# Single-bank PSUM tiles after the attention, and attention inputs in 128 partitions, in a linear-attention kernel with two MLPs

## The chip, the cores and the metric

The kernel runs on one core of a Trainium2 chip. The metric is the device time of one execution in microseconds (us). Three executions of the kernel before were timed; the profile comes from one more.

## The reference

Inputs: q, k, v of shape (4, 8, 576, 64), a scale g_norm of 64, and four weight matrices; all float32. Cut to what is computed:

```
kv  = einsum('bhsd,bhse->bhde', k, v)
o   = einsum('bhsd,bhde->bhse', q, kv)
x   = o / sqrt(mean(o*o, -1) + 1e-6) * g_norm      # as (2304 tokens, 512)
h   = x @ w_in;   h = softplus(h);        x = h @ w_out     # 512 -> 2048 -> 512
h   = x @ w_in2;  h = max(0.01*h, h);     out = h @ w_out2  # 512 -> 2048 -> 512
```

## The kernel before

**Attention.** There are four batches of 576 positions and four head pairs each, so 16 units. For a unit u, `load(u)` issues three DMAs from SP that bring q, k and v of two heads into `lda`, six neighbouring positions a partition in 96 partitions (`PQ = 96`, `R6 = 6`), in a ring of four buffers (`NLD = 4`). `T(u)` copies q into another order (`qp`, L372 to L376), transposes it in six pieces on TensorE (L419), forms k^T v of both heads in twelve small matmuls (L426), and evacuates both (`kvm` L436, `qt` L451 to L453). `O(u)` multiplies `qt` by `kvm` (L467) and copies the result into `xy` (L475, L477). `norm(b)` and `X(u)` scale a batch once its four pairs are there (L495 to L552).

**The MLPs.** Each of the two matrix products of each MLP is done as seven block products on sums of blocks (a Strassen-like scheme), with every operand split into a high and a low part, so that a block product is six matmuls. `product` (L820) does the first product of an MLP in pieces of six 384-column matmuls, `piece` (L1077, 256 columns; L1082, 384 columns) the second. `plain` (L910) does the first few blocks without the scheme, while the attention still runs. ScalarE and VectorE evacuate each piece: L1127, L1134, L1139, L841 and L835 after `product`, L699, L694 and L1093 after `piece`; L849 and L854 split the results for the next product.

**PSUM.** The eight banks of 512 float32 are allocated as four tiles `pw0` to `pw3` of 1024 columns, two banks each, for the whole kernel. `ps[0]` to `ps[7]` are the halves of these. `product` writes U into bank 0 or 1, V into bank 2 and W into bank 3 (`u_bank`); in `after`, L1139 copies U into W. `piece` writes banks 4 and 5, or 6 and 7. So two banks of one tile are in use for different pieces at the same time.

**What sets the order.** A planner (`Plan`) gets every operation with its cost by engine, the bank or the part of a buffer that it reads and writes (banks as keys `("ps", 0)` to `("ps", 7)`), and a due time; it makes a list schedule, and the code is emitted in that order, engine by engine. The waits between engines are added afterwards by the tile framework from what each instruction reads and writes in its tiles; they don't come from the planner's keys.

Of the kernel before, what the change touches and what calls it, by code (L numbers as in the profile page):

```python
# [133 lines left out]
def linear_attention_two_mlps(  # L134
# [32 lines left out]
    nc = tc.nc  # L167
# [6 lines left out]
    R6 = 6  # L174
    PQ = S // R6
# [168 lines left out]
    both = mstp.tile([P, 4, 8], F32, name="both")  # L344
    nc.gpsimd.memset(ones, 0.0)
# [47 lines left out]
    def load(u):
        b, hp = u // NPAIR, u % NPAIR
        hs = slice(2 * hp, 2 * hp + 2)
        for nm, src in (("q", q), ("k", k), ("v", v)):
            def fn(e, nm=nm, src=src):
                nc.sync.dma_start(
                    out=lda[nm][u % NLD],
                    in_=src[b, hs].rearrange("h (p r) d -> p h r d", r=R6),  # L400
                )

            op({"S": 0.93}, fn, (), [(nm, u % NLD)])

# [52 lines left out]
    o_, s_of = pw[2][:, 0:S], pw[2][:, S:S + HS]  # L457
# [33 lines left out]
    def norm(b):  # L491
        def f_s(e):
            for w in range(NB):
                for c in range(4):
                    nc.tensor.matmul(  # L495
                        s_of[32 * c:32 * (c + 1), :], ones[:, 6 - 2 * w:38 - 2 * w],
# [4 lines left out]
        sk, rk = [("ps", 5)], [("rs", b % 2)]  # L501
# [3 lines left out]
            lambda e: nc.scalar.activation(fa, s_of, AF.Ln, bias=eps_b, scale=2.0 ** -SHIFT / D),  # L505
# [7 lines left out]
        for w, (x, s0, o0) in enumerate(  # L513
            ((s_of, D * EPS, ALU.add), (fm, 1.0 / D, ALU.mult), (fm, -3.0, ALU.add))
# [23 lines left out]
    def X(u):  # L538
# [10 lines left out]
        op({"PE": 0.28}, f_b, [("rs", b % 2), ("pick",)], RK)  # L549
# [10 lines left out]
    def decode_w(F, which, a_reg):  # L560
# [22 lines left out]
        op({"S": (1.65, 1.4)[which]}, f_l, after_loads if (which, f) < (1, GF) and which else (), rk)  # L583
# [754 lines left out]
```

## Time and profile before

| | before |
|---|---|
| timed, median of 3 (us) | 847.48 (846.77 to 848.55) |
| the profiled execution's own time (us) | 847.53 |
| its span, first to last instruction (us) | 845.7 |
| TensorE matmul busy (us) | 802.2 |
| TensorE weight load busy (us) | 757.1 |
| VectorE / ScalarE busy (us) | 679.0 / 538.2 |
| mean granted TensorE clock | 0.988 |

A matmul's end is modelled in this profile, so the matmul row can look busy across part of a wait; the weight loads of the same engine have a row of their own (PEld). An idle time is given in brackets before the group that it precedes, with what ended it.

### The profile page before, as it was taken

The numbers are of one execution on the slowest core, as the hardware profiler recorded it, in microseconds if no ns is written. First come the engines' busy times: TensorE is split into PE (matmuls) and PEld (weight loads), VectorE is DVE, ScalarE is ACT, GpSimd is POOL, SyncE is SP. The second block draws the span as 40 slices with busy tenths as digits, with TensorE's granted clock in tenths as the row PEclk, the third lists the DMA queues.
The fourth block names the chain that finished last, engine by engine and source line by source line (L and its number), as shares of the span: only waits on it lengthen the run. The fifth ranks groups of instructions, "written<-read, shape, count | busy, mean of one in ns | idle before, by whom it ended". The sixth has DMA issues, their size and how long they took to land. (4 is left out here: it accounts for less than half of the span.)

```text
span 845.7 us, 13740 instructions
## 1 busy us (share of the span) xinstructions
PE 802.2 (95%) x5309; PEld 757.1 (90%) x5309; DVE 679.0 (80%) x1036; ACT 538.2 (64%) x883; POOL 41.0 (5%) x38
## 2 busy tenths in 40 slices
PE   7899799899999999999999999999999999999996
PEld 6677799898999999999998988998999999999996
DVE  3785899898888987886798998898889876876565
ACT  2587679778667675764467787686577554454441
POOL 2340620000000000000000000000000000000000
PEclk9999799999999999999999999999999999999999
DMA  9995448476854874754676959774865752563814
GB/s 250 269 260 193 193 180 321 177 247 251 327 209 186 311 254 164 289 198 155 247 269 223 349 187 404 273 266 151 331 216 187 295 206 104 213 211 107 280 39 112
DMA packets 71250, 192.53 MB, mean 228 GB/s; under 512 B 5520, under 2 KB 45456, under 8 KB 71184
## 3 DMA queue, kind: packets, MB, share of 16 engines
q1 hardware_dynamic: 69504, 190.86, 64.8%
q8 instruction: 41, 0.67, 0.3%
q10 hardware_dynamic: 1680, 0.79, 0.3%
q14 instruction: 25, 0.20, 0.1%
HBM read 152.31 MB, written 39.32 MB: 227 GB/s over the span
## 5 line engine op out<-in xcount | busy, mean ns | idle before, releaser
L820 PE MATMUL pw<-ra 128*128 128x384 f32 x1932 | 391.2, 337 | 9.7 <-ACT pw L1139 6.9
L820 PEld LDWEIGHTS pw<-ra 128*128 128x128 f32 x1932 | 332.5, 189 | 16.3 <-ACT pw L1139 10.5
L1077 PE MATMUL pw<-rb 128*128 128x256 f32 x1512 | 209.5, 284 | 9.5 <-DVE xy L699 6.9
L1082 PE MATMUL pw<-rb 128*128 128x384 f32 x1008 | 208.0, 341 | 9.0 <-DVE xy L699 3.8
L1077 PEld LDWEIGHTS pw<-rb 128*128 128x128 f32 x1512 | 195.2, 189 | 22.3 <-DVE xy L699 17.2
L1082 PEld LDWEIGHTS pw<-rb 128*128 128x128 f32 x1008 | 176.3, 189 | 19.4 <-DVE xy L699 11.0
L699 DVE TENSOR_TENSOR xy<-pw,xy 128x384 f32<-128x384 f32 (+2 forms) x247 | 134.1, 549 | 73.6 <-PE pw L1077 50.2
L849 ACT ACTIVATE rb<-mf 128x768 fp32r<-128x768 f32 x154 | 129.5, 845 | 78.5 <-PE pw L1077 41.0
L854 DVE TENSOR_TENSOR rb<-mf,rb 128x768 fp32r<-128x768 f32 x154 | 148.0, 962 | 21.6 <-ACT rb L849 21.1
L934 DVE TENSOR_TENSOR mf<-mf 128x768 f32<-128x768 f32 x68 | 65.7, 975 | 2.8 <-ACT mf L835 2.2
L1127 ACT ACTIVATE mf<-pw 128x384 f32<-128x384 f32 x92 | 44.8, 489 | 35.3 <-PE pw L820 34.3
L1134 DVE TENSOR_TENSOR mf<-pw,mf 128x384 f32<-128x384 f32 x92 | 50.7, 553 | 11.5 <-PE pw L820 10.0
L1139 ACT ACTIVATE pw<-pw 128x384 f32<-128x384 f32 x46 | 22.0, 479 | 25.6 <-PE pw L820 25.1
L835 ACT ACTIVATE mf<-mf 128x768 f32<-128x768 f32 x26 | 21.9, 843 | 18.7 <-DVE mf L1134 18.6
L1093 ACT ACTIVATE pw<-pw 128x384 f32<-128x384 f32 (+2 forms) x44 | 21.0, 478 | 16.1 <-PE pw L1077 9.0
L996 ACT ACTIVATE rb<-rc 128x512 fp32r<-128x512 f32 x44 | 27.3, 626 | 2.0 <-PE pw L1077 0.8
L999 DVE TENSOR_TENSOR rb<-rc,rb 128x512 fp32r<-128x512 f32 x42 | 28.4, 683 | 0.3 <-ACT rb L996 0.3
L841 ACT ACTIVATE mf<-mf 128x768 f32<-128x768 f32 x24 | 20.2, 841 | 8.6 <-DVE mf L1134 8.5
L694 ACT ACTIVATE xy<-pw 128x384 f32<-128x384 f32 (+2 forms) x40 | 18.8, 480 | 10.1 <-PE pw L1077 4.5
L841 ACT ACTIVATE mf<-pw 128x384 f32<-128x384 f32 x32 | 15.7, 491 | 11.5 <-PE pw L820 11.1
L612 ACT ACTIVATE sqr<-mf 128x512 uint16<-128x512 uint16 x29 | 22.6, 780 | 0.0
L475 ACT ACTIVATE xy<-pw 128x576 f32<-128x576 f32 x14 | 9.0, 646 | 21.3 <-PE pw L467 21.2
(120 smaller groups left out, 740.0 us busy)
## 6 DMA issues: line engine op xcount, KB each, us to landing
ra<-xscr SPq DMA_DIRECT2D x131, 768.0 KB, 6.3
xscr<-ra SPq DMA_DIRECT2D x30, 768.0 KB, 4.5
mf<-in_moe_w_in_dram SPq DMA_DIRECT2D x18, 512.0 KB, 5.9
mf<-in_moe_w_out_dram SPq DMA_DIRECT2D x18, 512.0 KB, 4.9
lf<-in_moe_w_in_dram SPq DMA_DIRECT2D x14, 512.0 KB, 6.2
lf<-in_moe_w_out_dram SPq DMA_DIRECT2D x14, 512.0 KB, 5.4
xscr<-xy SPq DMA_DIRECT2D x8, 768.0 KB, 6.3
qa<-in_q_dram SPq DMA_DIRECT2D x16, 288.0 KB, 8.7
```

Source lines behind the costliest of these rows:

```text
L699: {"D": t_d(n)}, lambda e: nc.vector.tensor_tensor(dst, src, dst, ALU.add),
L820: nc.tensor.matmul(o, w_[:, a, c:c + P], e_[:, b, kk, :], start=(not on and which < 2 and kk == 0 and n == 0), stop=(kk == 1 and n == 2), ...
L841: lambda e: nc.scalar.activation(dst(), src(), AF.Prelu, alpha=0.01),
L849: {"A": t_a(n)}, lambda e: nc.scalar.activation(g[:, 0, :, :], c.ap, AF.Copy),
L854: lambda e: nc.vector.tensor_tensor(g[:, 1, :, :], c.ap, g[:, 0, :, :].bitcast(F32), ALU.subtract),
L934: lambda e: nc.vector.tensor_tensor(to.ap, x.ap, y.ap, ALU.subtract),
L996: op({"A": t_a(512)}, lambda e: nc.scalar.activation(w_[:, 0], src(), AF.Copy), sk, hk)
L999: lambda e: ENG[e].tensor_tensor(w_[:, 1], src(), w_[:, 0].bitcast(F32), ALU.subtract), sk + hk, lk,
L1077: nc.tensor.matmul(y[:, 256 * (j % 2):256 * (j % 2 + 1)], G_[:, a, m, js], w_[:, b, m, :], **flags)
L1082: nc.tensor.matmul(y[:, :BN], w_[:, a, m, js], G_[:, b, m, :], **flags)
L1127: {"A": t_a(BN)}, lambda e: nc.scalar.activation(c[:, m, :], src, AF.Copy),
L1134: lambda e: nc.vector.tensor_tensor(c[:, m, :], src, c[:, m, :], ALU.add),
```

## The change

1. **PSUM.** `pw0` to `pw3` stay for the attention alone. They are allocated in two pools, `psb` with `pw1` and `psa` with the other three. When the last unit that uses `pw1` is done (`U_H = 10`), `psb` is closed and banks 2 and 3 become tiles `ps2` and `ps3` of one bank each; when the attention's last norm is done, `psa` is closed and the other six banks become `ps0`, `ps1` and `ps4` to `ps7`. A new tile waits for the users of the old tile that it lies on. What reads a bank in the MLPs looks the tile up when it is emitted (`lambda` and `src()` in place of slices made at the start).
2. **q, k and v.** 512 of the 576 positions of a batch lie in 128 partitions, four to a partition; the 64 that are left come for all eight heads of a batch in one DMA for each of q, k and v (`ldr`, 64 partitions, 256 bytes a row; the other 64 partitions are set to zero once). A unit has four transposes and one for the left rows (`f_tl`), and ten small matmuls in place of twelve. The ring has five buffers.
3. **O and the stores.** In odd batches the 64 left positions stand first in `o_`, so that a matmul's output stays within a bank; the rows of the result are stored in runs of 128 and 64 in place of 96.
4. **The planner's costs** of the loads follow the new sizes, and those of the weights' loads go from 1.65 and 1.4 to 1.47 and 1.3. The block products' costs are as before.

The diff, cut to its core (`psum` slices that became lookups are shown once):

```
-    R6 = 6
-    PQ = S // R6
+    RL = S - 4 * P
...
-        rows = out[b * S:(b + 1) * S, :].rearrange("(p r) d -> r p d", r=R6)
-        runs += [(PQ, rows[r]) for r in range(R6)]
+        rows = out[b * S:b * S + 4 * P, :].rearrange("(p r) d -> r p d", r=4)
+        left = (RL, out[b * S + 4 * P:(b + 1) * S, :])
+        runs += [left] * (b % 2) + [(P, rows[r]) for r in range(4)] + [left] * (1 - b % 2)
...
-    psum = ctx.enter_context(tc.tile_pool(name="psum", bufs=1, space=PSUM))
-    pw = ring(psum, "pw", 4, [P, 1024])
-    ps = [t[:, c:c + 512] for t in pw for c in (0, 512)]
+    psa = tc.tile_pool(name="psa", bufs=1, space=PSUM, side="right")
+    psb = tc.tile_pool(name="psb", bufs=1, space=PSUM)
+    psap, psbp = psa.__enter__(), psb.__enter__()
+    pw = [(psbp if i == 1 else psap).tile([P, 1024], F32, name=f"pw{i}") for i in range(4)]
+    ps = [None] * 8
+
+    def banks(old, name, which, **kw):
+        old.__exit__(None, None, None)
+        p = ctx.enter_context(
+            tc.tile_pool(name=name, bufs=1, space=PSUM, reuse_waits="tile", **kw)
+        )
+        for i in which:
+            ps[i] = p.tile([P, 512], F32, name=f"ps{i}")
...
-    NLD = 4
+    NLD = 5
     NB = 4
     HS = S // 4
-    lda = {nm: ring(attp, nm + "a", NLD, [PQ, 2, R6, D]) for nm in "qkv"}
-    qp = ring(attp, "qp", 2, [PQ, R6, 2, D])
+    lda = {nm: ring(attp, nm + "a", NLD, [P, 2, 4, D]) for nm in "qkv"}
+    ldr = {nm: ring(attp, nm + "r", 2, [P, H, D]) for nm in "qkv"}
+    qp = ring(attp, "qp", 2, [P, 4, 2, D])
...
+    for t, e_ in enumerate((nc.vector, nc.gpsimd)):
+        for n in "qkv":
+            e_.memset(ldr[n][t][RL:], 0.0)
...
-                    in_=src[b, hs].rearrange("h (p r) d -> p h r d", r=R6),
-                )
-
-            op({"S": 0.93}, fn, (), [(nm, u % NLD)])
+                    in_=src[b, hs, 0:4 * P, :].rearrange("h (p r) d -> p h r d", r=4),
+                )
+
+            first = "qkv".index(nm) - 60.0 if u == 0 else None
+            op({"S": 0.74}, fn, (), [(nm, u % NLD)], due=first)
+        if hp == 0:
+            for nm, src in (("q", q), ("k", k), ("v", v)):
+                def fn(e, nm=nm, src=src):
+                    nc.sync.dma_start(
+                        out=ldr[nm][b % 2][:RL], in_=src[b, :, 4 * P:S, :].rearrange("h p d -> p h d")
+                    )
+
+                op({"S": 0.6}, fn, (), [(nm + "r", b % 2)])
...
         t = i if u < U_H else 0
         k0, k1 = ("ps", 2 * t), ("ps", 2 * t + 1)
-        qc = pw[t][:, 32:32 + S]
-        kv = pw[t][:, 32 + S:32 + S + D]
+        qc, kv = pw[t][:, 0:S], pw[t][:, 5 * P:5 * P + D]
         ka, va = lda["k"][u % NLD], lda["v"][u % NLD]
+        ql, kl, vl = (ldr[nm][b % 2] for nm in "qkv")
 
         def f_t(e):
-            for r in range(R6):
-                nc.tensor.transpose(
-                    qc[:, r * PQ:(r + 1) * PQ], qp[i][:, r, :, :], ident[0:PQ, 0:PQ]
-                )
+            for r in range(4):
+                nc.tensor.transpose(qc[:, r * P:(r + 1) * P], qp[i][:, r, :, :], ident)
+
+        def f_tl(e):
+            nc.tensor.transpose(pw[t][:, 4 * P:5 * P], ql[:, h2, :], ident)
 
         def f_kv(e):
-            for r in range(R6):
+            for r in range(5):
                 for h in range(2):
+                    k_, v_ = (x[:, 2 * hp + h, :] for x in (kl, vl)) if r == 4 else (
+                        x[:, h, r, :] for x in (ka, va)
+                    )
                     nc.tensor.matmul(
-                        kv[h * D:(h + 1) * D, :], ka[:, h, r, :], va[:, h, r, :],
-                        start=(r == 0), stop=(r == R6 - 1), tile_position=(0, h * D),
+                        kv[h * D:(h + 1) * D, :], k_, v_, start=(r == 0), stop=(r == 4),
+                        tile_position=(0, h * D),
                     )
 
-        op({"PE": 0.5}, f_t, [("qp", i)], [k0, k1])
-        op({"PE": 0.75}, f_kv, [("k", u % NLD), ("v", u % NLD)], [k1])
+        op({"PE": 0.44}, f_t, [("qp", i)], [k0])
+        op({"PE": 0.11}, f_tl, [("qr", b % 2)], [k1])
+        op(
+            {"PE": 0.7}, f_kv,
+            [("k", u % NLD), ("v", u % NLD), ("kr", b % 2), ("vr", b % 2)], [k1],
+        )
...
+    def o_of(b):
+        return pw[2][:, 4 * P - RL:] if b % 2 else pw[2][:, 0:S]
+
+    def s_of(b):
+        return pw[2][:, 0:HS] if b % 2 else pw[2][:, S:S + HS]
...
-            for c0, c1 in ((0, 512), (512, S)):
-                nc.tensor.matmul(
-                    o_[:, c0:c1], kvm[i], qt[i][:, c0:c1], start=True, stop=True
-                )
+            at = b % 2 * RL
...
-        sk, rk = [("ps", 5)], [("rs", b % 2)]
+        sk, rk = [("ps", 5 - b % 2)], [("rs", b % 2)]
...
-        op({"S": (1.65, 1.4)[which]}, f_l, after_loads if (which, f) < (1, GF) and which else (), rk)
+        op({"S": (1.47, 1.3)[which]}, f_l, after_loads if (which, f) < (1, GF) and which else (), rk)
...
-        U, V, W = (ps[u_bank(s, x_)][:, :BN] for x_ in range(3))
+        U, V, W = (lambda x_=x_: ps[u_bank(s, x_)][:, :BN] for x_ in range(3))
...
+        banks(psa, "psc", (0, 1, 4, 5, 6, 7), side="right")
...
+        if i == U_H:
+            op({"N": 0.0}, lambda e: banks(psb, "psd", (2, 3)), (), [("ps", 2), ("ps", 3)])
...
+       + [("ps", i) for i in (0, 1, 4, 5, 6, 7)]
```

TensorE where the second MLP's second product begins (`pw2` and `pw3` hold banks 4 to 7, `pw0` and `pw1` banks 0 to 3). Before:

```order
L1065 MATMUL pw3_86<-rb_911 128x128 [waits DVE_49]
L1077 MATMUL pw2_85<-rb_911 128x256 [waits DVE_49]
L1077 MATMUL pw2_85<-rb_911 128x256 x11
L820 MATMUL pw1_84<-ra_74 128x384 [waits DMAHW4_49,DVE_49]
L820 MATMUL pw1_84<-ra_74 128x384 x5
L1077 MATMUL pw2_85<-rb_911 128x256 [waits Activation_49]
L1077 MATMUL pw2_85<-rb_911 128x256 x5
L820 MATMUL pw0_83<-ra_74 128x384 [waits DMAHW0_49]
```

Now, with the lines of the changed kernel (L864 is `product`, L1126 is `piece`):

```order
L1114 MATMUL ps6_978<-rb_879 128x128 [waits DVE_49]
L1126 MATMUL ps4_976<-rb_879 128x256 [waits DVE_49]
L1126 MATMUL ps4_976<-rb_879 128x256 x11
L864 MATMUL ps2_561<-ra_74 128x384 [waits DMAHW0_49,DVE_49]
L864 MATMUL ps2_561<-ra_74 128x384 x5
L864 MATMUL ps0_974<-ra_74 128x384 [waits DMAHW4_49,Activation_49]
L864 MATMUL ps0_974<-ra_74 128x384 x5
L1126 MATMUL ps5_977<-rb_879 128x256 [waits DVE_49]
```

The third piece of L1077 writes bank 5; before it waits for ScalarE (for L1093, which reads bank 4 of the same tile), now for VectorE, and a piece of the first product stands ahead of it.

SP's queue from the start, before (`qa`, `ka`, `va` are the ring of `load`):

```order
L398 DMA qa0_93<-in_q_dram 96x2x384
L398 DMA ka0_97<-in_k_dram 96x2x384
L398 DMA va0_101<-in_v_dram 96x2x384
L398 DMA qa1_94<-in_q_dram 96x2x384
L398 DMA ka1_98<-in_k_dram 96x2x384
L398 DMA va1_102<-in_v_dram 96x2x384
L398 DMA qa2_95<-in_q_dram 96x2x384
```

Now (`qr`, `kr`, `vr` hold the left rows):

```order
L412 DMA qa_96<-in_q_dram 128x2x256
L412 DMA ka_101<-in_k_dram 128x2x256
L412 DMA va_106<-in_v_dram 128x2x256
L422 DMA qr_111<-in_q_dram 64x8x64
L422 DMA kr_113<-in_k_dram 64x8x64
L422 DMA vr_115<-in_v_dram 64x8x64
L412 DMA ka_102<-in_k_dram 128x2x256
L412 DMA va_107<-in_v_dram 128x2x256
```

The three loads of left rows stand ahead of the second unit's, and the first unit needs all six.

## Rows read from the trace of the kernel before

**Rows 1.** Busy time of each engine: us (share of the span) xinstructions

```profile
PE 802.2 (95%) x5309; PEld 757.1 (90%) x5309; DVE 679.0 (80%) x1036; ACT 538.2 (64%) x883; POOL 41.0 (5%) x38
```

**Rows 2.** Timeline at the end: start us, us, engine, line, operation [idle before]

```profile
840.37 0.98 PE L1077 MATMUL pw<-rb 128*128 128x256 f32 x6 [0.52 <-DVE xy L699]
```

**Rows 3.** Waits of TensorE's matmuls: engine line <- releaser: us, times, longest us

```profile
PE pw L820 <- ACT pw L1139: 6.9, 10, 2.4
PE pw L1077 <- DVE xy L699: 6.9, 13, 0.8
PE pw L426 <- DMA va<-in_v_dram: 4.6, 5, 1.2
PE pw L1082 <- DVE xy L699: 3.8, 5, 1.4
PE pw L1082 <- DVE rb L854: 2.4, 2, 1.9
...
PE pw L1082 <- ACT xy L694: 1.3, 2, 1.0
```

**Rows 4.** Waits of the weight loads, same columns

```profile
PEld pw L1077 <- DVE xy L699: 17.2, 31, 1.1
...
PEld pw L820 <- DVE mf L1134: 2.3, 2, 1.8
```

**Rows 5.** Timeline near 610 us, columns as in the second group

```profile
607.46 1.59 PE L1077 MATMUL pw<-rb 128*128 128x256 f32 x12
...
608.89 1.21 PE L820 MATMUL pw<-ra 128*128 128x384 f32 x6
...
609.93 0.87 PE L1077 MATMUL pw<-rb 128*128 128x256 f32 x6
...
610.64 1.21 PE L820 MATMUL pw<-ra 128*128 128x384 f32 x6
...
611.65 0.68 DVE L699 TENSOR_TENSOR xy<-pw,xy 128x512 f32<-128x512 f32 x1
...
612.38 1.69 PE L1077 MATMUL pw<-rb 128*128 128x256 f32 x12 [0.53 <-DVE xy L699]
...
613.91 1.21 PE L820 MATMUL pw<-ra 128*128 128x384 f32 x6
```

**Rows 6.** Timeline near 100 us, same columns

```profile
100.35 1.34 PE L820 MATMUL pw<-ra 128*128 128x384 f32 x6 [2.36 <-ACT pw L1139]
```

**Rows 7.** Stretches: busy of PE, PEld, DVE, ACT, POOL; PEclk, DMA, GB/s

```profile
5.50:42.00 36.50, 29.74 (x362) 22.45 (x361) 20.15 (x37) 15.88 (x30) 8.95 (x8) 0.95 1.08 272
42.00:91.20 49.20, 46.44 (x467) 38.70 (x465) 33.99 (x58) 38.54 (x70) 14.88 (x11) 0.94 0.75 212
91.20:480.00 388.80, 372.99 (x2068) 358.16 (x2069) 339.92 (x496) 270.00 (x439) 14.24 (x7) 0.99 0.66 240
480.00:820.00 340.00, 329.83 (x2252) 315.43 (x2251) 267.53 (x411) 207.74 (x340) 0.00 (x0) 1.00 0.61 220
820.00:845.70 25.70, 19.14 (x150) 18.25 (x148) 15.78 (x28) 4.72 (x6) 0.00 (x0) 0.94 0.45 122
```

**Rows 8.** Wait of VectorE for TensorE, columns as in the third group

```profile
DVE xy L699 <- PE pw L1077: 50.2, 64, 1.8
```

**Rows 9.** Groups, first 92 us: operation xcount | busy us, mean ns | idle

```profile
L426 PE MATMUL pw<-va,ka 96*64 96x64 f32 x384 | 14.7, 226 | 4.6 <-DMA va<-in_v_dram 4.6
...
L419 PE MATMUL pw<-ident,qp 96*128 96x96 f32 x96 | 11.3, 255 | 2.5 <-ACT qt L451 0.9 <-POOL qp L376 0.8 <-ACT qp L372 0.4
...
L376 POOL TENSOR_SCALAR qp<-qa 96x768 f32<-96x768 f32 x7 | 5.8, 831 | 27.6 <-DMA qa<-in_q_dram 23.0 <-DVE kvm L436 2.8 <-DVE ra L677 1.8
```

**Rows 10.** Three more stretches, columns as in the seventh group

```profile
5.50:37.00 31.50, 24.74 (x320) 18.70 (x320) 15.18 (x31) 13.60 (x25) 6.46 (x7) 1.00 1.08 272
...
98.00:105.00 7.00, 2.71 (x10) 2.29 (x11) 7.00 (x7) 4.12 (x8) 4.44 (x2) 0.79 0.80 334
832.00:845.70 13.70, 7.99 (x63) 7.37 (x61) 5.61 (x13) 0.00 (x0) 0.00 (x0) 0.89 0.42 115
```

More of the change, by code (lines that the diff above doesn't have):

```diff
@@ L385, in fn @@
             if e == "A":
-                nc.scalar.activation(out, in_, AF.Copy)
+                nc.scalar.activation(out, in_(), AF.Copy)
             else:
-                nc.vector.tensor_copy(out, in_)
+                nc.vector.tensor_copy(out, in_())
         return op({"A": t_a(n), "D": t_d(n)}, fn, [], [("ps", bank), *writes])
@@ L463, in O @@
         cols = slice(b * S, (b + 1) * S)
+        o_ = o_of(b)
         def f_o(e):
-            for c0, c1 in ((0, 512), (512, S)):
-                nc.tensor.matmul(
-                    o_[:, c0:c1], kvm[i], qt[i][:, c0:c1], start=True, stop=True
-                )
+            at = b % 2 * RL
+            nc.tensor.matmul(
+                o_[:, at:at + 4 * P], kvm[i], qt[i][:, 0:4 * P], start=True, stop=True
+            )
+            at = (1 - b % 2) * 4 * P
+            nc.tensor.matmul(
+                o_[:, at:at + RL], kvm[i], qt[i][:, 4 * P:S], start=True, stop=True
+            )
         op({"PE": 0.98}, f_o, [("kvm", i), ("qt", i)], OK)
@@ L491, in norm @@
     def norm(b):
+        s_ = s_of(b)
         def f_s(e):
@@ L513, in norm @@
         for w, (x, s0, o0) in enumerate(
-            ((s_of, D * EPS, ALU.add), (fm, 1.0 / D, ALU.mult), (fm, -3.0, ALU.add))
+            ((s_, D * EPS, ALU.add), (fm, 1.0 / D, ALU.mult), (fm, -3.0, ALU.add))
         ):
@@ L547, in f_b @@
                 )
-        op({"PE": 0.28}, f_b, [("rs", b % 2), ("pick",)], RK)
+        op({"PE": 0.47}, f_b, [("rs", b % 2), ("pick",)], RK)
         op(
@@ L692, in to_xy @@
                 {"D": t_d(n), "A": t_a(n)},
-                lambda e: nc.vector.tensor_copy(dst, src) if e == "D"
-                else nc.scalar.activation(dst, src, AF.Copy),
+                lambda e: nc.vector.tensor_copy(dst, src()) if e == "D"
+                else nc.scalar.activation(dst, src(), AF.Copy),
                 [("ps", bank)], xk,
@@ L698, in to_xy @@
             op(
-                {"D": t_d(n)}, lambda e: nc.vector.tensor_tensor(dst, src, dst, ALU.add),
+                {"D": t_d(n)}, lambda e: nc.vector.tensor_tensor(dst, src(), dst, ALU.add),
                 [("ps", bank)] + xk, xk,
@@ L900, in plain, with o @@
         for m in range(2):
-            o = ps[2 + m][:, :BN]
+            def o(m=m):
+                return ps[2 + m][:, :BN]
             for j in range(2):
@@ L1044, in to_y, with src @@
                 dst = xy[:, 2 * a:2 * a + 2, c0:c0 + n].rearrange("p a (j n) -> p j a n", n=P)
-                src = ps[bank][:, (j0 % 2) * 256:(j0 % 2) * 256 + 2 * n]
-                src = src.rearrange("p (j a n) -> p j a n", a=2, n=P)
+                def src():
+                    y = ps[bank][:, (j0 % 2) * 256:(j0 % 2) * 256 + (j1 - j0) * 256]
+                    return y.rearrange("p (j a n) -> p j a n", a=2, n=P)
                 kcs, n = [2 * a, 2 * a + 1], 2 * n
@@ L1049, in to_y @@
                 kcs, n = [2 * a + j0], BN
-                dst, src = xy[:, kcs[0], c0:c0 + BN], ps[bank][:, :BN]
+                dst, src = xy[:, kcs[0], c0:c0 + BN], lambda: ps[bank][:, :BN]
             to_xy(dst, src, n, g % NG == 0 and i in ((5, 1, 2, 6) if pre else (0, 1, 2, 6)), bank, xyk(kcs, c0, n // len(kcs)))
@@ L1057, in piece @@
             bank = (6 if i in (1, 3, 5) else 4) + (j // 2 if tokens else j)
-            y = ps[bank]
             new = i < 2 or not pre and i == 5
@@ L1063, in fn @@
             def fn(e):
+                y = ps[bank]
                 if widens:
@@ L1092, in piece @@
                         {"A": t_a(n)},
-                        lambda e: nc.scalar.activation(ps[bank + 2][:, :n], y[:, :n], AF.Copy),
+                        lambda e: nc.scalar.activation(
+                            ps[bank + 2][:, :n], ps[bank][:, :n], AF.Copy
+                        ),
                         [("ps", bank)], [("ps", bank + 2)],
@@ L1126, in copy @@
             op(
-                {"A": t_a(BN)}, lambda e: nc.scalar.activation(c[:, m, :], src, AF.Copy),
+                {"A": t_a(BN)}, lambda e: nc.scalar.activation(c[:, m, :], src(), AF.Copy),
                 bank, ck(c, m),
@@ L1133, in plus @@
                 {"D": t_d(BN)},
-                lambda e: nc.vector.tensor_tensor(c[:, m, :], src, c[:, m, :], ALU.add),
+                lambda e: nc.vector.tensor_tensor(c[:, m, :], src(), c[:, m, :], ALU.add),
                 bank + ck(c, m), ck(c, m),
@@ L1138, in after @@
         if i == 0:
-            op({"A": t_a(BN)}, lambda e: nc.scalar.activation(W, U, AF.Copy), bu, bw)
+            op({"A": t_a(BN)}, lambda e: nc.scalar.activation(W(), U(), AF.Copy), bu, bw)
         elif i == 1:
@@ L1149, in after @@
         elif i == 5:
-            act(s, lambda: cA[:, 1, :], lambda: W, BN, bw, ck(cA, 1))
+            act(s, lambda: cA[:, 1, :], W, BN, bw, ck(cA, 1))
         else:
-            act(s, lambda: cA[:, 0, :], lambda: U, BN, bu, ck(cA, 0))
+            act(s, lambda: cA[:, 0, :], U, BN, bu, ck(cA, 0))
     def attention_done(e):
@@ L1182, in warm @@
         for _ in range(N_WARM):
-            nc.tensor.transpose(ps[7][:, 0:P], ident, ident)
+            nc.tensor.transpose(pw[3][:, 512:512 + P], ident, ident)
     op({"PE": 0.0}, warm, (), [("ps", 7)], due=-100.0)
@@ L1229, in linear_attention_two_mlps @@
        + [(t, i) for t in ("qp", "qt", "kvm") for i in range(2)]
-       + [(t, i) for t in "qkv" for i in range(NLD)])
+       + [(t, i) for t in "qkv" for i in range(NLD)]
+       + [(t + "r", i) for t in "qkv" for i in range(2)])
     op({"N": 0.0}, norm_done, (), granules("rc", "lf")
+       + [("ps", i) for i in (0, 1, 4, 5, 6, 7)]
        + [("sq", i) for i in range(NB)] + [("rs", i) for i in range(2)]
```

12 lines of the change are left out of this document (6 added, 6 removed).

## The prediction, made before the changed kernel ran

> **What bounds the kernel now.** I read the busy times first, then the waits of the busiest engine, then one stall closely, then the stretches. TensorE's matmuls are busy 802.2 of 845.7 us, VectorE 679.0 [rows 1]: the kernel is bound by TensorE, and only what lets TensorE lose less, or work less, can move its time. From 91.2 us to the last matmul (the last group starts at 840.37 and takes 0.98, so to 841.35 [rows 2]) it works at the MLPs; before that lies the attention.
>
> What TensorE waits for in the MLPs is nearly all PSUM. Seven rows of its waits name a reader of PSUM, from L820 behind L1139 (6.9 us) to L1082 behind L694 (1.3 us); they add up to 23.5 us [rows 3]. The two waits for an operand, L1082 behind L854, are 2.4 us, and the loads of v cost 4.6 us in the attention. The weight loads show the same stalls larger: six rows, from 17.2 to 2.3 us, 83 waits, 46.7 us in all [rows 4].
>
> The timeline shows which is right. Undisturbed, six matmuls of L820 take from 608.89 to 609.93, 1.04 us, and twelve of L1077 from 607.46 to 608.89, 1.43 us. At the stall six of L820 start at 610.64 and the next group only at 612.38, 1.74 us later, and its twelve take 1.53 us [rows 5]. So the stall costs 0.70 + 0.10 = 0.80 us, where the matmul row shows 0.53 idle: 0.27 us more than is shown, since the modelled end covers a part and the second matmul after a stall is late too. The Trainium skill, Perfetto Trace Analysis, Identifying the Most-Contended Engine, says that matmul busy time is no good measure of the room that is left, and to take the weight loads' busy share; this stall agrees. By the matmul row the room in PSUM waits would be 23.5 us, by the weight loads 46.7.
>
> **Whose bank is it?** In this stall TensorE writes bank 7 (the last third of a `piece`), and what it waits for is L699, which reads bank 6 from 611.65 to 612.33 [rows 5]: the other half of `pw3`. The long one at 100.35 is V, bank 2, behind L1139, which writes W, bank 3; 2.36 us [rows 6]. The planner keeps banks apart, but the waits are made per tile, and a tile has two banks. In the built program, 327 of TensorE's waits in the two products name a user of the other bank of the pair, 74 one of its own bank; in the changed program none and 441. Going through the idle times, 22.5 of the 23.5 us lie behind the other bank; the rest is behind the bank's own reader and stays.
>
> **Part 1, single-bank tiles: what goes.** 22.5 us of shown idle, and 0.27 us for each of 83 waits, 22.4 us: 45 us (46.7 by the weight loads alone). I share it out by the weight loads' idle: 388.8 - 358.2 = 30.6 us from 91.2 to 480, 340 - 315.4 = 24.6 from 480 to 820, 21.35 - 18.25 = 3.1 from there to the last matmul [rows 7]. That makes 23.6, 19.0 and 2.4 us.
>
> **What is late next.** A stall that goes brings TensorE to its next need sooner. VectorE is the engine that could then be late: it is busy 339.9 of 388.8 us in the first stretch and 267.5 of 340 in the second [rows 7]. With the stalls gone these shares would be 339.9/365.2 = 93% and 267.5/321 = 83%. That is near the limit in the first. At its beginning it is at the limit: VectorE is busy 7.00 of 7.00 us from 98 to 105 [rows 10], so that the 2.36 us at 100.35 come back as a longer wait for L854. On the other side VectorE itself waits 50.2 us for TensorE's L1077 [rows 8], partly for a write to the bank beside the one that it reads, and these waits go as well. I take 0.6 of the first stretch, 0.8 of the second and 0.65 at the end: 14.2 + 15.2 + 1.6 = 31.0 us. The bounds are 0.3 of all, if VectorE's order holds TensorE up (13.5), and all (45).
>
> **Waits that are added.** A bank that is handed over waits for the users of the old tile. Banks 2 and 3 do so before the first L910, which now stands later; about twelve matmuls of L910 at 0.174 us (1.04 for six [rows 5] for the same width) move behind the last norm: TensorE does them either way, and they cost only if it stood idle before, at most 2 us. I take 0.
>
> **Part 2, q, k and v: TensorE.** The small matmuls of a unit go from 24 passes to 20; 384 passes are 14.7 us of busy time [rows 9], so 64 fewer are 2.4 us less. The transposes go from 6 x 96 to 5 x 128 columns, 11% more of 11.3 us (96 transposes) [rows 9], 1.2 us more. Of the difference, 1.2 us, I count half, since TensorE is busy 46.4 of 49.2 us in the second half of the attention but 29.7 of 36.5 in the first [rows 7]: -0.6 us. The copies of q shrink from 768 to 512 columns, 0.83 to 0.55 us on GpSimd [rows 9]; they are waited for now and then, and I put this at nothing, with GpSimd's 27.6 us of idle before them as the cover. Six new memsets of 64 x 512 lie beside the first loads and TensorE's warming transposes.
>
> **Part 2: the loads.** The attention's first part is bound by them: from 5.5 to 37 us the DMA engines are at 1.08 of full and move 272 GB/s [rows 10]. The whole of q, k and v, 14.16 MB, takes 52 us at that. Of the changed loads, 12.58 MB go to 128 partitions. The nearest row for those is the stretch from 98 to 105, 334 GB/s at a share of 0.80 (larger packets) [rows 10]. So they take 37.7 us at 334, or 46.2 at 272 as now: 8.5 us less, or no change. The left rows, 1.57 MB in packets of 256 bytes, have no row. The stores at the end, 512 bytes a packet, move 115 GB/s at a share of 0.42 [rows 10], 274 at a full one: 5.7 us for the left rows. If a packet of 256 bytes takes as long as one of 512, it is 11.5: 5.7 more than now. So all loads take 8.5 us less to 5.7 more. TensorE waits for them until 35 us, so some 0.6 of it counts: -5.1 to +3.4. I take -2, nearer to the first, because twelve of the fifteen loads of a batch are of the 128-partition kind. The Trainium skill, SBUF — State Buffer, Door 1: The DMA port swizzle, gives 328 GB/s for 128 partitions and 196 for 64, at 1 MiB. By these 38.4 + 8.0 = 46.4 us, 5.6 less than now (an estimate), which at 0.6 would be -3.4; that the 64-partition rows are slow speaks against them, and no row here shows such a load.
>
> The first unit now needs six loads, 1.15 MB, where it needed three, 0.86 MB: about 1 us at 272 GB/s for the first small matmuls; by the fourth unit the bytes are equal, and nothing remains of it.
>
> **Part 3 and 4: stores and order.** 23 stores replace 42. All but the last few lie beside other work, and the end is as before: last piece, two L699, a store and its landing, 845.7 - 841.35 = 4.3 us. I take 0. The planner's new order moves pieces of the two products against each other by one place here and there; its price is unknown in sign, and within the bounds above.
>
> **Sum.** 847.53 (the profiled execution's own time; 0.05 above the median, and 1.8 above its span) - 31.0 - 0.6 - 2.0 = 813.9. Predicted: 814 us. The range's ends: all 45 us, both gains of the attention with the loads at -3: 847.5 - 45 - 3.6 = 799; half of the forecast's 31 and nothing else: 832.
>
> **The rivals.**
> *The stalls come back as others.* VectorE's order holds TensorE as the banks do now; 0.3 of part 1 is left: 847.5 - 13.5 + 0 = 834, and 833 to 845 as its span. For it: 93% in the first stretch. Against: VectorE waits 50.2 us for L1077 alone [rows 8], so it is mostly the one that is early.
> *All of the weight loads' idle goes.* In the MLPs it is 30.6 + 24.6 + 3.1 = 58.3 us [rows 7], of which 46.7 lie in the wait rows for PSUM. If the next group's weights always load ahead once nothing holds them, the other 11.6 go too: 847.5 - 58.3 - 2.6 = 787. Against: VectorE's 679.0 us [rows 1] would be 86% of 787, with never an idle time in the wrong place. The Trainium skill, Perfetto Trace Analysis, Identifying the Most-Contended Engine, would count all of this idle as room; no row here shows a stretch without any.
> *The change does not do what it says*: the waits go by bank, but what ends last is the same piece's own evacuation: no change, 847.5. Against it stands the stall at 612.38, where the bank's own reader had long been done.
> *Slower, by the opening.* TensorE's clock was granted at 0.95 and 0.94 in the two stretches of the attention [rows 7], and at 0.99 to 1.00 in the MLPs. If the left rows arrive late in every batch, TensorE waits in each unit and the grant stays at the 1.2 GHz level from 42 to 91.2: 46.4 us of work at 0.94 become 87 at 0.5, 41 more, and 5.7 for the loads: 847.5 - 31 + 47 = 863. It decides from the point at which the opening loses more than 33 us. Against: five buffers in the ring, and the loads are no more bytes than before.
>
> **How the numbers follow.** Chances: the forecast with its range 0.79; stalls that come back 0.09; all idle gone (below 799) 0.04; no change 0.04; slower 0.04. The range 799 to 832 so leaves 0.21 out; I set its upper end at 834, the time of the first rival, which brings the chance outside to 0.2 or less. A measurement of this kernel can tell about 0.2% (1.7 us) from no change. Faster 0.79 + 0.09 + 0.04 = 0.92, within 0.2% 0.04, slower 0.04.
>
> **What would show it.** Right, if in the changed profile the waits of the second product for L699 and of the first for L1139 are a third of these or less, the weight loads' busy share rises from 90% to some 93%, and the stretch of the MLPs is about 31 us shorter. The loads: 5.5 to 37 us at more than 272 GB/s. Wrong, if the MLPs' waits for L699 and L1139 are gone and waits for L854, L849 or the own bank of the same sum stand in their place, or if the attention ends later than 91 us with a lower granted clock.

## The result, and the profile after

| kernel | median us | ratio to before, 95% interval |
|---|---|---|
| before | 847.12 (846.63 to 848.55, 4 runs) | |
| changed | 792.26 (790.78 to 793.49, 4 runs) | 0.9349 [0.9326, 0.9372] |

The change takes 54.9 us off where 33.5 were forecast; the time lies 7 us below the range. The profiled execution (790.78 us, span 789.0) is read in the order of the prediction. The page's busy times, which answer [rows 1] (PE is TensorE's matmuls, PEld its weight loads, DVE VectorE, ACT ScalarE, POOL GpSimd):

```profile
PE 770.0 (98%) x5229; PEld 752.0 (95%) x5229; DVE 684.0 (87%) x1044; ACT 531.3 (67%) x877; POOL 42.0 (5%) x41
```

The longest waits of TensorE's matmuls, which answer [rows 3] (engine, line, what released it: us, times, longest us):

```profile
PE ps L956 <- ACT mf L400: 2.6, 1, 2.6
PE pw L588 <- DVE xy L596: 2.0, 2, 1.2
PE pw L1235 <- POOL ident masks.py:199: 2.0, 1, 2.0
PE ps L1131 <- DVE rb L898: 1.7, 1, 1.7
PE ps L1131 <- DVE rb L1045: 1.2, 1, 1.2
PE pw L454 <- DMA vr<-in_v_dram: 1.0, 1, 1.0
```

The waits of the second product for the readers of `xy` (L699, now L743) and of the first for L1139 (now L1190) are not a third of what they were, as forecast, but gone. All of the rows above lie before 100 us. The stretches, which answer [rows 7] (us; busy of PE, PEld, DVE, ACT, POOL; PEclk, DMA share, GB/s):

```profile
5.50:42.00 36.50, 32.45 (x403) 23.84 (x402) 22.28 (x45) 21.95 (x42) 9.36 (x11) 1.00 1.07 324
42.00:91.20 49.20, 43.39 (x375) 36.36 (x374) 42.31 (x59) 36.77 (x65) 16.97 (x13) 1.00 0.64 209
91.20:480.00 388.80, 385.13 (x2252) 383.10 (x2251) 358.88 (x532) 286.21 (x472) 11.20 (x6) 1.00 0.69 257
480.00:789.00 309.00, 305.51 (x2187) 305.16 (x2185) 256.25 (x399) 185.09 (x301) 0.00 (x0) 1.00 0.61 225
```

From 91.2 to 480 the weight loads are idle for 5.7 us, where it was 30.6. VectorE is busy 92% of this stretch, about the share that the prediction took for the limit, and TensorE waits for it only at the stretch's start (the 1.7 and 1.2 us above). The timeline where [rows 5] had the stall now reads as undisturbed work (start us, us, engine, line, operation):

```profile
605.51 1.59 PE L1126 MATMUL ps<-rb 128*128 128x256 f32 x12
606.94 1.21 PE L864 MATMUL ps<-ra 128*128 128x384 f32 x6
607.98 0.87 PE L1126 MATMUL ps<-rb 128*128 128x256 f32 x6
608.69 1.21 PE L864 MATMUL ps<-ra 128*128 128x384 f32 x6
```

Twelve of 256 columns take 1.43 us, six of 384 take 1.04, six of 256 take 0.71, one behind the other. VectorE's own wait, which answers [rows 8], has fallen from 50.2 to:

```profile
DVE xy L743 <- PE ps L1126: 21.8, 49, 1.1
```

**Where the 55 us went.** All the traces hold the same 4,549 matmuls of the MLPs, so I counted them by their start times; the 96th and the 301st serve as marks for the opening. The table, worked out from the profiled executions, gives the start of the 96th, of the 301st and of the last, and the time from the 301st to the last.

| kernel | 96th | 301st | last | 301st to last |
|---|---|---|---|---|
| before | 93.5 | 139.0 | 841.1 | 702.1 |
| changed | 85.0 | 129.3 | 785.2 | 655.9 |
| banks_alone | 90.8 | 135.9 | 791.6 | 655.7 |
| loads_alone | 86.7 | 133.9 | 833.0 | 699.0 |
| vector_small | 90.6 | 141.1 | 798.2 | 657.1 |
| old_costs | 95.8 | 139.4 | 794.6 | 655.2 |
| vector_splits | 81.2 | 120.9 | 776.2 | 655.4 |

So 46.2 us come from the MLPs behind their first 300 matmuls, and 9.7 from what lies before: 8.5 of these are there at the 96th already. The rows below the first two are the experiments that settle which part did it.

### The profile page after: what moved, and what is told of

It is laid out like the page before. It is cut to its first block, busy times and chain, and to the rows that moved or that the text cites. A ratio compares the mean times of both kernels' runs of the same rounds, so it can differ in the third digit from the quotient of the medians.

```text
span 789.0 us, 13537 instructions
## 1 busy us (share of the span) xinstructions
PE 770.0 (98%) x5229; PEld 752.0 (95%) x5229; DVE 684.0 (87%) x1044; ACT 531.3 (67%) x877; POOL 42.0 (5%) x41
## 4 chain that ended last, share of the span: by engine, by line
PE 89%; DVE 6%; DMA 2%; ACT 1%; issue 1%; SPq 1%; DVEq 0%; ACTq 0%
PE ps L864 41%; PE ps L1126 23%; PE ps L1131 20%; PE pw L505 1%; PE pw L454 1%; DMA xscr<-xy 1%; DVE rb L898 1%; DMA ra<-xscr 1%; DMA va<-in_v_dram 1%; DVE rc L801 1%; PE ps L956 1%; PE pw L588 1%; PE pw L443 1%; DVE xy L596 1%; PE pw L539 0%
## 5 line engine op out<-in xcount | busy, mean ns | idle before, releaser
L864 PE MATMUL ps<-ra 128*128 128x384 f32 x1932 | 388.0, 336 | 0.7 <-ACT mf L1178 0.5
L864 PEld LDWEIGHTS ps<-ra 128*128 128x128 f32 x1932 | 333.0, 189 | 1.9 <-ACT mf L1178 1.0
L1131 PE MATMUL ps<-rb 128*128 128x384 f32 x1008 | 201.9, 334 | 3.0 <-DVE rb L898 1.7
L1126 PE MATMUL ps<-rb 128*128 128x256 f32 x1512 | 204.1, 282 | 0.0
L1126 PEld LDWEIGHTS ps<-rb 128*128 128x128 f32 x1512 | 198.2, 189 | 0.1
L1131 PEld LDWEIGHTS ps<-rb 128*128 128x128 f32 x1008 | 176.9, 188 | 3.9 <-DVE rb L898 2.1
L898 DVE TENSOR_TENSOR rb<-mf,rb 128x768 fp32r<-128x768 f32 x154 | 149.5, 971 | 22.5 <-ACT rb L893 21.4
L743 DVE TENSOR_TENSOR xy<-ps,xy 128x384 f32<-128x384 f32 (+2 forms) x247 | 134.6, 548 | 33.1 <-PE ps L1126 21.8
L1178 ACT ACTIVATE mf<-ps 128x384 f32<-128x384 f32 x92 | 44.6, 487 | 27.1 <-PE ps L864 26.5
L1185 DVE TENSOR_TENSOR mf<-ps,mf 128x384 f32<-128x384 f32 x92 | 50.7, 553 | 11.1 <-PE ps L864 9.5
L1190 ACT ACTIVATE ps<-ps 128x384 f32<-128x384 f32 x46 | 22.2, 482 | 23.5 <-PE ps L864 23.3
L1045 DVE TENSOR_TENSOR rb<-rc,rb 128x512 fp32r<-128x512 f32 x44 | 30.8, 707 | 0.0
L1142 ACT ACTIVATE ps<-ps 128x384 f32<-128x384 f32 (+2 forms) x44 | 21.1, 480 | 6.9 <-PE ps L1131 3.4
L956 PE MATMUL ps<-ra 128*128 128x384 f32 x96 | 19.3, 344 | 2.6 <-ACT mf L400 2.6
L885 ACT ACTIVATE mf<-ps 128x384 f32<-128x384 f32 x32 | 15.7, 490 | 9.1 <-PE ps L864 8.9
```

The source lines that it names most:

```text
L743: {"D": t_d(n)}, lambda e: nc.vector.tensor_tensor(dst, src(), dst, ALU.add),
L864: nc.tensor.matmul(o, w_[:, a, c:c + P], e_[:, b, kk, :], start=(not on and which < 2 and kk == 0 and n == 0), stop=(kk == 1 and n == 2), ...
L885: lambda e: nc.scalar.activation(dst(), src(), AF.Prelu, alpha=0.01),
L898: lambda e: nc.vector.tensor_tensor(g[:, 1, :, :], c.ap, g[:, 0, :, :].bitcast(F32), ALU.subtract),
L1045: lambda e: ENG[e].tensor_tensor(w_[:, 1], src(), w_[:, 0].bitcast(F32), ALU.subtract), sk + hk, lk,
L1126: nc.tensor.matmul(y[:, 256 * (j % 2):256 * (j % 2 + 1)], G_[:, a, m, js], w_[:, b, m, :], **flags)
```

## Experiments

**Whose banks.** Four kernels take the change apart. `banks_alone` puts the pools of single-bank tiles into the kernel before and leaves the loads, the units and the costs as they were (the planner then puts some operations of VectorE and ScalarE, from 89 to 230 us, in other places); the other three are the changed kernel with two-bank tiles again for some banks, in the same order on every engine:

```
         for i in which:
-            ps[i] = p.tile([P, 512], F32, name=f"ps{i}")
+            if i // 2 in (0, 1, 2, 3):      # loads_alone; first_pairs: (0, 1); second_pairs: (2, 3)
+                if i % 2 == 0:
+                    t = p.tile([P, 1024], F32, name=f"pp{i}")
+                    ps[i], ps[i + 1] = t[:, 0:512], t[:, 512:1024]
+            else:
+                ps[i] = p.tile([P, 512], F32, name=f"ps{i}")
```

`banks_alone`: 

> The kernel before with the first part of the change alone: single-bank tiles after the attention; loads, units and costs of the attention as before, and TensorE's order as before but for one place. Theory A (the waits by pairs are nearly the whole gain: about 50 us of the 55, since each stall cost its shown idle, a late second matmul and a bit of the clock, and VectorE had room): 797 us, 794 to 801. Theory B (the prediction's 31 us for the pairs was right, the other 24 us came from the loads, the new order and the clock of the opening): 816 us, 812 to 820.

`loads_alone`: 

> The changed kernel with two-bank tiles in all of it: the pools are handed over at the same places, but every tile again holds two banks; each engine's order is that of the changed kernel. Theory A: 842 us (792 + 50), 838 to 846, with TensorE's waits in the two products again behind users of the other bank. Theory B: 823 us, 819 to 827.

`first_pairs`: 

> The changed kernel with banks 0 to 3 (the first product's) in two-bank tiles and banks 4 to 7 single. In the trace of before 12.8 of the 46.7 us of idle weight loads behind PSUM users lay in the first product. Theory 1 (the stalls of the two products add up, each at some 1.07 times its weight-load idle): 792 + 14 = 806 us, 802 to 810. Theory 2 (a stall that goes in one product comes back in the other, so that one kind of pair alone costs about as much as both): above 820 us. Theory 3 (one kind alone is taken up by slack): below 798 us.

`second_pairs`: 

> The changed kernel with banks 4 to 7 (the second product's) in two-bank tiles and banks 0 to 3 single. In the trace of before 33.9 of the 46.7 us lay in the second product. Theory 1 (they add up): 792 + 36 = 828 us, 823 to 833, and with the run before this one its extra time makes that of the kernel with all pairs. Theory 2 (one kind alone costs as much as both): above 836 us. Theory 3 (slack takes it up): below 812 us.

| kernel | median us | ratio to before, 95% interval |
|---|---|---|
| banks_alone | 799.07 | 0.9425 [0.9402, 0.9449] |
| loads_alone | 838.11 | 0.9881 [0.9858, 0.9904] |
| first_pairs | 808.26 | 0.9529 [0.9501, 0.9556] |
| second_pairs | 828.13 | 0.9767 [0.9740, 0.9794] |

Theory A holds, and theory 1 of the two kinds of pairs. Put into the kernel before, single banks are worth 847.63 - 799.07 = 48.6 us, of which 46.4 lie behind the 301st matmul in the traces; taken out of the changed kernel with every engine's order kept, 838.11 - 792.26 = 45.9. By kind of pair it is 16.0 and 35.9 us, 51.9 together: they nearly add up, 6 us overlap.

The waits of the weight loads from 95 us on read this price off. First `loads_alone`, then `first_pairs`, then `second_pairs`, the largest rows of each:

```profile
PEld pp L1131 <- DVE xy L748: 17.1, 30, 1.5
PEld pp L1136 <- DVE xy L748: 13.8, 26, 1.7
PEld pp L869 <- ACT pp L1195: 5.7, 8, 1.2
```

```profile
PEld pp L869 <- ACT pp L1195: 9.7, 12, 2.0
PEld pp L869 <- ACT rc L884: 1.9, 4, 0.7
```

```profile
PEld pp L1131 <- DVE xy L748: 16.4, 31, 1.1
PEld pp L1136 <- DVE xy L748: 14.3, 28, 1.7
```

All such rows add up to 51.0, 19.6 and 42.8 us; the changed kernel has 3.5. The differences are 47.5, 16.1 and 39.3 us where the times differ by 45.9, 16.0 and 35.9. The matmuls' own rows of `loads_alone` add up to 24.2 us against 1.9, half of the price. The Trainium skill, Perfetto Trace Analysis, Identifying the Most-Contended Engine, says to judge TensorE's room by the weight loads' busy share and not by the matmuls'; these runs agree to within 3.5 us.

**Does VectorE hold TensorE up?** The prediction kept 31 of 45 us because VectorE would be 93% busy. `vector_small` gives VectorE one more copy behind each split of L898 (L854 before: the low part of an operand), `vector_large` two:

```
+        def f_low(e):
+            nc.vector.tensor_tensor(
+                g[:, 1, :, :], c.ap, g[:, 0, :, :].bitcast(F32), ALU.subtract
+            )
+            for _ in range(1):                  # vector_large: range(2)
+                nc.vector.tensor_copy(pad, ident[:, 0:96])      # vector_large: 0:120
```

`vector_small`: 

> The changed kernel with one more VectorE copy of 128x96 behind each of the 168 splits of L898, in the same order; 93 of them lie between 91 and 480 us, about 0.17 us each (an estimate from the rows of 128x144 and 128x32), so VectorE's need there goes from 359 to some 375 of 388.8 us, 96%. Theory A (the prediction's factors failed because VectorE at 92% does not hold TensorE up): within 3 us of the changed kernel, 792 to 795. Theory B (near 93% VectorE's order is the limit, as the factor 0.6 had it, so that 0.4 or more of what is put on it comes through): 6 us or more, above 798.

`vector_large`: 

> The changed kernel with two more VectorE copies of 128x120 behind each split of L898: about 0.38 us for each of the 93 between 91 and 480 us, 35 us, so VectorE's need there goes to 394 us, over the 388.8 that there are. Theory A (only what goes beyond TensorE's own time counts): 5 us over in this stretch, more by waits at some places: 797 to 806. Theory B (0.4 or more of the first 16 us and nearly all of the rest come through): 815 or more.

Measured: 799.72 us, 0.9436 [0.9410, 0.9463], and 816.44 us, 0.9642 [0.9612, 0.9671]. By the time alone theory B has both. By the place it has not. From 125 to 300 us, in the changed kernel, `vector_small` and `vector_large` (columns as in the stretches above):

```profile
125.00:300.00 175.00, 175.00 (x1011) 175.00 (x1011) 164.81 (x256) 134.89 (x225) 0.00 (x0) 1.00 0.72 267
```

```profile
125.00:300.00 175.00, 175.00 (x1011) 175.00 (x1010) 168.56 (x295) 135.74 (x225) 0.00 (x0) 1.00 0.71 262
```

```profile
125.00:300.00 175.00, 172.88 (x987) 170.48 (x986) 171.54 (x329) 131.74 (x221) 0.00 (x0) 1.00 0.70 254
```

With VectorE busy 168.56 of 175 us, 96%, TensorE loses nothing: matmuls and weight loads fill the stretch. In `vector_large`, at 98%, the weight loads lose 4.5 us. That share is of a stretch with 987 matmuls in place of 1,011; for 1,011 VectorE would need 171.54 x 1011/987 = 175.7 us (an estimate), more than the 175 that there are. From the 301st matmul on, `vector_small` is 1.2 us longer than the changed kernel, `vector_large` 14.3. So near 93% there was no holding back, nor at 96%; TensorE lost time where VectorE's need was about all of the stretch. What lies between was not run.

The other 6.2 us of `vector_small` lie between the 96th and the 301st matmul, where VectorE has no room in the changed kernel (busy 33.80 of 33.80 us from 91.2 to 125). (A further 5.6 us of its profiled execution, which at 803.80 us was the longest of six, had been lost before the first added copy started, with the clock at 0.84 from 5.5 to 16 us.) Three lines of its timeline, of GpSimd, VectorE and TensorE, show the longest wait among them:

```profile
110.13 2.52 POOL L767 TENSOR_TENSOR ra<-rc,ra 128x768 fp32r<-128x768 f32 x1
...
110.91 1.81 DVE L902 COPY pad<-ident 128x96 f32<-128x96 f32 x1
...
113.24 4.07 PE L1133 MATMUL ps<-rb 128*128 128x384 f32 x12 [4.44 <-DVE xy L738]
```

The added copy, 0.20 us by the median, takes 1.81 while GpSimd has a split in hand; the evacuation behind it (L738) starts late, and TensorE waits 4.44 us, some 1.6 of them for the copy. Its next twelve matmuls take 3.9 us to the following start where 2.1 is usual, at the 1.2 GHz level. Only this longest execution has a trace; where the median's 7.5 us lie was not seen.

**What is in the opening.** Four kernels. `v_left_out` and `before_v_left_out` take loads away, `ring_four` the fifth buffer, `old_costs` three of the planner's new numbers (the second pair below, for the product that spreads the norm, belongs to the change as well):

```
+                if nm == "v" and u >= NLD:      # v_left_out, before_v_left_out
+                    return
...
-    NLD = 5
+    NLD = 4                                     # ring_four
...
-            op({"S": 0.74}, fn, (), [(nm, u % NLD)], due=first)
+            op({"S": 0.93}, fn, (), [(nm, u % NLD)], due=first)     # old_costs, three edits
...
-        op({"PE": 0.47}, f_b, [("rs", b % 2), ("pick",)], RK)
+        op({"PE": 0.28}, f_b, [("rs", b % 2), ("pick",)], RK)
...
-        op({"S": (1.47, 1.3)[which]}, f_l, ...)
+        op({"S": (1.65, 1.4)[which]}, f_l, ...)
```

`v_left_out`: 

> The changed kernel without the loads of v in 128 partitions from the sixth unit on (old values of the ring are used; this changes what is computed): 2.9 MB less, 8.9 us of transfer at 324 GB/s. Theory A (the loads still set the opening, 0.6 of their time counts, as the prediction had it): 5 us faster, 785 to 789. Theory B (with the new loads TensorE and the evacuations set the opening): within 1.5 us of the changed kernel.

`before_v_left_out`: 

> The kernel before without the loads of v from the fifth unit on (old values of the ring are used; this changes what is computed): 3.5 MB less, 13 us of transfer at 272 GB/s. Theory A (in the kernel before the loads set the opening, and the changed loads took them out of the way; that is where the 7 to 9 us outside the MLPs' stalls came from): 6 to 9 us faster than before, 838 to 841. Theory B (the opening of before was held by TensorE, the evacuations or the clock): within 2 us of before, 845 to 849.

`ring_four`: 

> The changed kernel with four buffers in the ring of q, k and v in place of five. Theory A (the opening gained by the transfer rate alone): within 1.5 us of the changed kernel. Theory B (the loads' lead of five units is part of the gain): 2 to 4 us slower.

`old_costs`: 

> The changed kernel with the planner's costs of before for the loads of q, k and v (0.93), of the weights (1.65 and 1.4) and for the product that spreads the norm (0.28), so that the order is another while all work is the same. Theory A (the new order is part of the 7 to 9 us that the loads alone gained): 2 to 5 us slower than the changed kernel, 794 to 797. Theory B (the order is worth nothing, the price is 0 as the prediction took it): within 1.5 us, 791 to 794.

| kernel | median us | ratio to before, 95% interval |
|---|---|---|
| v_left_out | 791.32 | 0.9347 [0.9325, 0.9368] |
| before_v_left_out | 844.05 | 0.9967 [0.9953, 0.9982] |
| ring_four | 796.26 | 0.9399 [0.9376, 0.9422] |
| old_costs | 800.59 | 0.9450 [0.9422, 0.9477] |

In the changed kernel the loads set nothing (8.9 us less of transfer are worth 0.9 us, within the spread). In the kernel before, 13 us less of transfer are worth 2.7 us, 0.2 of it and not 0.6; its wait for v all but went and the time with it did not:

```profile
PE pw L428 <- DMA va<-in_v_dram: 0.6, 1, 0.6
```

So neither theory of that run holds as it stood. The surprise is `old_costs`: the same work in another order is 8.3 us longer, more than theory A asked for. It is also no better than `banks_alone` (800.59 and 799.07, intervals overlapping): with the old costs, the new loads, the units in 128 partitions and the fifth buffer together gain nothing that can be measured. With the new costs they do: `loads_alone`, which has them and two-bank tiles, takes 9.5 us less than the kernel before (838.11 and 847.63).

The table of start times shows where the order tells. `old_costs` is 10.8 us behind the changed kernel at the 96th matmul and 10.1 at the 301st, so the loss lies in the attention: its last matmul starts at 89.0 us in place of 80.8. From 42 to 91.2 us in `old_costs` (the changed kernel's row stands further up):

```profile
42.00:91.20 49.20, 44.44 (x376) 36.54 (x377) 36.59 (x63) 33.92 (x63) 12.43 (x11) 0.90 0.52 174
```

VectorE is not full there (36.59 of 49.20 us, and 42.31 in the changed kernel), and TensorE's clock was granted at 0.90 where it was 1.00. Two of TensorE's waits in the attention, in `old_costs` first and then in the changed kernel:

```profile
PE pw L588 <- DVE xy L596: 3.9, 4, 1.0
PE pw L505 <- DVE fm L562: 3.2, 2, 2.9
```

```profile
PE pw L588 <- DVE xy L596: 2.0, 2, 1.2
PE pw L505 <- DVE fm L562: 0.6, 1, 0.6
```

Both are waits for small operations of the norm on VectorE (L562, L596), and they differ by 4.5 us. The lower clock costs at most (1.00 - 0.90) x 49.2 = 4.9 us more (an estimate, for a TensorE that always has work). Together they can account for the 8.2 us by which the attention ends later; no run separates them. Which of the three numbers does it was not tried. `ring_four` changes the order as well (4.0 us), so the fifth buffer's own worth is not separated from the order's.

**A version that is faster than both.** From 91.2 to 125 us VectorE is busy throughout, in the kernel before and in the changed one:

```profile
91.20:125.00 33.80, 28.17 (x141) 26.67 (x142) 33.80 (x35) 23.06 (x39) 14.24 (x7) 0.89 0.50 190
```

```profile
91.20:125.00 33.80, 30.36 (x164) 28.88 (x163) 33.80 (x40) 24.60 (x42) 11.20 (x6) 0.95 0.61 236
```

Its operations are long where GpSimd works. In the changed kernel, lines of GpSimd and VectorE:

```profile
89.09 4.45 POOL L766 TENSOR_TENSOR ra<-rc,ra 128x768 fp32r<-128x768 f32 x2 [3.25 <-ACT ra L771]
```

```profile
89.53 2.33 DVE L1028 TENSOR_TENSOR mf<-rc,mf 128x512 f32<-128x512 f32 x1
91.78 2.58 DVE L898 TENSOR_TENSOR rb<-mf,rb 128x768 fp32r<-128x768 f32 x1
94.29 1.75 DVE L1045 TENSOR_TENSOR rb<-rc,rb 128x512 fp32r<-128x512 f32 x1
```

Alone, L1028 takes 0.68 us, L898 0.95, L1045 0.68. A split takes GpSimd 2.2 us and costs VectorE more than a microsecond; VectorE does one in 0.95. Between 40 and 125 us of this trace, 14 operations of VectorE take over 0.2 us longer than the shortest of their line and shape, 15.2 us in all, and each lies beside an operation of GpSimd. So two kernels give the splits to VectorE:

```
-            split_part(xe[at], src, sk, "DP")
+            split_part(xe[at], src, sk, "D")        # and the other calls of split_part: x_splits
...
-            {"D": t_d(512), "P": t_p(512)} if g == 0 else {"D": t_d(512)},
+            {"D": t_d(512)},                        # vector_splits has this too
```

`vector_splits`: 

> The changed kernel with the 13 splits (L766, L1045) that GpSimd does before 105 us given to VectorE. In the changed kernel's trace VectorE's L898 takes 2.04 and 2.58 us where GpSimd has a split in hand, 0.95 elsewhere, and TensorE's last stalls (2.6, 1.7, 1.2 us, and 3.4 us at the half clock) lie between 85 and 101 us. Theory A (the splits on GpSimd cost VectorE about as much as doing them itself, 0.6 to 0.95 us each, and more at the latency): 3 to 6 us faster than the changed kernel, 786 to 789. Theory B (VectorE is full there, and 11 us more on it delay the MLPs' start): 3 us or more slower, above 795.

`x_splits`: 

> The changed kernel with the nine splits of L766 given to VectorE, while L1045 may stay on GpSimd. Theory A: 2 to 4 us faster, 788 to 790. Theory B: 2 us or more slower, above 794.

Measured: 784.26 us, 0.9265 [0.9242, 0.9288], and 785.42 us, 0.9275 [0.9255, 0.9295]. Both beat the changed kernel, by 8.0 and 6.8 us, a little more than theory A had. Without GpSimd's splits the same stretch of `vector_splits` is at the full clock throughout:

```profile
91.20:125.00 33.80, 31.65 (x177) 30.35 (x177) 33.80 (x47) 27.33 (x45) 0.00 (x0) 1.00 0.63 249
```

VectorE finishes 47 operations where the changed kernel finishes 40, in the same 33.80 us, and none between 40 and 125 us is lengthened any more: 15.2 us saved for some 11.3 us of added splits (9 of 0.95 and 4 of 0.68 us). The Trainium skill, Perfetto Trace Analysis, Optimizing Scalar/DVE Operations, says that VectorE and GpSimd share a read port of SBUF, so that offloading between the two might not help. It did not help here; the port itself no run shows. The gain of 7 to 8 us cannot be put on the splits alone: the planner also made another order of VectorE's and ScalarE's operations from 38 us on, and an order can be worth as much (`old_costs`). A kernel with the splits moved and the order kept was not run.

## Why the prediction was wrong in size

**Right.** TensorE bounds the kernel; the stalls in the MLPs come from the other bank of the pair; the banks' waits, not the loads, are the bulk of it. The 45 us of part 1, from 22.5 us of shown idle and 0.27 us for each of 83 waits, are near what the runs give: 45.9 to 48.6. The 0.27 us are from one stall, so that the sum comes so near is in part luck; the weight loads' own 46.7 us say the same without it.

**The step that failed: the factors 0.6, 0.8 and 0.65 on these 45 us.** They stood for VectorE, which near 93% would hold TensorE up, and left 31.0 us. It did not: 46.2 us went behind the 301st matmul alone, and with VectorE at 96% TensorE still lost nothing. A share of the busy time, and the worry that it is high, carried a factor of a third with no row behind it; [rows 8], 50.2 us of VectorE waiting for TensorE, was the row that spoke against it, and I gave it too little weight. The rival in which all the weight loads' idle goes (787 us, chance 0.04) had the mechanism, down to stretches without any idle; its 58.3 us went but for about 6 (5.7 from 91.2 to 480 us).

**The order: taken at 0, measured at 8.3.** The prediction looked at the order of the two products alone (pieces moved "by one place here and there") and took it at 0. That holds behind the 301st matmul, where `loads_alone` and before differ by 3 us and `banks_alone`, `old_costs`, `vector_splits` and the changed kernel by less than 1. It fails in the attention, where `old_costs` is 8.2 us late at the end: TensorE waits 4.5 us longer there for two small operations of the norm, on a VectorE that is not full, and works at a lower clock. Which place in the order does it is open. `old_costs` is one other order; that the new costs made a better one was not foreseen, and so it is luck.

**The loads and TensorE's work: -2.6, not to be measured by themselves.** The rate came as forecast, 324 GB/s in place of 272, near the 334 of the row that I took: 14.16 MB take 43.7 us at that in place of 52, so that the transfer's 8.5 us are there. What was wrong is that 0.6 of it counts: it was 0.2 in the kernel before (2.7 of 13 us), and with the old costs the opening did not end earlier for it (301st matmul at 139.4 us, 139.0 before).

**The clock.** I took nothing for it. From 42 to 91.2 us it was granted at 0.94 [rows 7] and now at 1.00, from 91.2 to 125 at 0.89 and now at 0.95. In the changed kernel it was at 0.50, the 1.2 GHz level, from 97.2 to 100.5 us, behind stalls of TensorE of 2.6, 1.7 and 1.2 us, and six matmuls of L864 are busy for 1.93 us there where 1.20 is usual. So a stall in the opening can cost more than its idle. This may be part of what the order and the banks gained there; it was not measured by itself, and it does not settle the time: `banks_alone` was granted 1.00 in all three stretches up to 125 us, `old_costs` 1.00, 0.90 and 0.90, and their times do not differ measurably. `vector_small`'s executions go from 797.21 us at a mean of 0.995 to 803.80 at 0.989.

**Waits that come back.** The 2.36 us at 100.35 were to come back as a longer wait for VectorE's split. They did so in small part: the matmuls' waits for splits are 2.9 us (L898 1.7, L1045 1.2) where they were 2.4 (L854 [rows 3]). The plain blocks that move behind the last norm were taken at 0; one of them waits 2.6 us for its bank (L956 behind L400) where the like wait was 1.0. The rival with a slower opening is excluded: the left rows land in 6.3 to 6.5 us (medians) beside the others' 5.3 to 5.5, and the attention's last matmul starts at 80.8 where it was 91.0.

**The sum as it should have been**, from runs: 847.5 - 48.6 (single banks) - 8.3 (order) + 1.5 (loads, units and ring with the old costs, within the spread) = 792.1. Each term is the difference of two runs on the way from one kernel to the other, so it is bound to add up; what the runs show is the sizes.

## What to carry to other kernels

Price a stall of TensorE by the weight loads' idle behind it, and discount it only if a row shows the engine that would be late next; a busy share of 92 to 96% on that engine was no such row here. A planner's order is worth a run of its own: three cost numbers made 8.3 us here, and not where VectorE was full but in the attention. Where an engine is at 100%, ask what runs beside it: moving 13 splits from GpSimd to VectorE, with the order that followed from it, was worth 8.0 us. If waits go by tile, give each bank that is used on its own a tile of its own.

## What the runs showed that was not expected

- VectorE's operations take two and a half times as long and more beside GpSimd's two-input operations: 2.33 for 0.68 us, 2.58 for 0.95, 1.75 for 0.68, and the added one-input copy 1.81 for 0.20.
- VectorE at 96% busy (168.56 of 175 us) lets TensorE run without a gap; where it needed about all of the time (171.54 us for 987 matmuls in place of 1,011) the weight loads lost 4.5 us.
- With 64-partition loads in packets of 256 bytes among them, the loads moved 324 GB/s at a share of 1.07, where 96 partitions had 272 at 1.08. The 128-partition loads alone were not timed.
- An equal amount of work in another order changed the time by 8.3 us, and the loss is there at the 96th of 4,549 matmuls (95.8 and 85.0 us).
